# Infini-attention beside an FNet block on one core: value loads later in SyncE's order, chunk loads spread over the value tiles, the low memory products behind eight projection terms

## The chip, the cores and the metric

The kernel runs on 1 core of one Trainium2 chip. The metric is the device time of one execution in microseconds; the median of 3 runs before the change is 1089.74 us (1086.66 to 1097.31). One further execution was profiled; every duration below comes from it.

## The reference

Two independent blocks are computed from 2048 x 576 inputs in float32, and their results stand side by side in the output.

```python
# A: attention with a compressive memory: 32 heads of 18 columns, 4 segments of 512 rows
q, k, v = x @ wq, x @ wk, x @ wv
for s in range(4):
    logits = qs @ ks.T * scale + mask          # the mask adds -1e9 where key column > query row
    a_dot  = softmax(logits) @ vs
    a_mem  = (phi(qs) @ M) / (phi(qs) @ z + 1e-6)
    o      = g * a_mem + (1 - g) * a_dot       # g = sigmoid(beta), one per head
    M, z   = M + phi(ks).T @ vs, z + sum(phi(ks))
out_A = concat(o) @ wo
# B: real part of a DFT over the hidden and then the sequence axis
a, b  = x @ hid_re.T, x @ hid_im.T
out_B = seq_re @ a - seq_im @ b
```

## The kernel before, in words

**Numbers as halves.** Float32 operands are split into a high part (an ACT copy to the matmul type) and a low part (a subtraction on DVE or POOL), and a product is made of three matmuls: high x low, high x high, low x high. So most loads are followed by a split before TensorE (PE) can use them. All engines run the program in the order in which it was written (the schedule is manual). Every DMA is issued by SyncE (SP), from one queue and in order: a DMA that has to wait for a buffer or for data holds back all the DMAs behind it.

**The order written by hand.** `later(n, fn)` puts a call n ticks ahead of now, and `tick()` (line 85) runs what is due. In the first stage a tick comes after each projection tile and each value tile. In the second stage a tick comes after each *piece* of attention, of which there are eight in each step p of `attention()` (line 804). After each tick the loop at line 864 also emits dense work until its share of the total has caught up.

**First stage, segments s = 0 to 3 (lines 433 to 477).** `open_qk(s)` runs the first four projection tiles: for s > 0 terms 0 to 5 of all four tiles, then `accumulate(3)`, then terms 6 to 13 of all four. `accumulate(3)` adds the last 128 rows of the segment before to the memory: three products (high keys x high values, high x low, low x high) of five matmuls each. Then `memory()` copies the memory out of PSUM on ACT and masks it on POOL. Nine calls of `project_qk` follow; each stores its tile to DRAM one or two ticks later. Then come four value tiles j: `project_v(s, j)` on PE, an evacuation to `vs` (two buffers, `vs_bufs[j % 2]`), a store `vd<-vs`, and for s > 0 `lookup(s, j)` with a store `amd<-am` (`am` has one buffer). In the last segment the loop also starts the second stage: from n = 6 on the stacks of group 0 are loaded, and the first chunks of the dense work are loaded by `c_load` (four `craw` buffers) and split by `c_cut` (chunk 0 at j = 1, chunk 1 at j = 2; later ones by `chunk(n)`, which loads chunk n + 4 and splits chunk n + 2).

**Second stage.** PE alternates attention and dense work (B's two DFTs: `hidden` and `sequence`). Attention takes 32 groups G of four heads; a group needs two steps p, so 16 pieces. With the ticks counted from the start of `attention()`, group G's events, all on SP unless another engine is named, are:

| tick | event |
|---|---|
| 16G - 15 to 16G - 13 | the twelve loads `qs<-qd` and `ks<-kd` of group G (`stack_load`, called in step 2(G - 1)) |
| 16G + 13 | PE: the last `pv` of group G - 2, last reader of its value tile |
| 16G + 15 | `vst<-vd`, the value tile of group G (two buffers, so it waits for that `pv`) |
| next piece | `ptt<-hl`, a DMA transpose (`f_turn`; one in each step p) |
| 16G + 16 | PE: transposes the row maxima of group G (`trm`); ACT copies them to `mt` |
| 16G + 17 | `md<-mt`, stores them to DRAM; then the twelve loads of group G + 2, up to tick 16G + 19 |
| 16G + 22 | `qs<-md`, loads the maxima back as extra rows of `qs` |
| 16G + 24 | PE: the first `t_fill` of group G (line 737), which reads those rows |
| 16G + 35 | PE: the first `pv` of group G, which reads the value tile |

The tick of the value load is `later(lag, values)` in `stack_load` (line 418), called at tick 16(G - 1) with a lag of 31. Group 0 has a lag of 99 of its own and is loaded before `attention()` starts. At the end, A's output projection runs on PE (lines 884 to 900).

Of the kernel before, what the change touches and what calls it, by code (L numbers as in the profile page):

```python
# [36 lines left out]
def infini_attention_and_fnet(ctx: ExitStack, tc: tile.TileContext, xT, wqk, w8, wv, wo, beta, xtT, cT, hT, out):  # L37
# [44 lines left out]
    def later(n, fn, *a):  # L82
        due.setdefault(clock[0] + n, []).append((fn, a))

    def tick():
        clock[0] += 1
        for fn, a in due.pop(clock[0], ()):
            fn(*a)  # L88
# [12 lines left out]
    def load_x(s, k):  # L101
        t = sb.tile([P, L], F32, name="raw", tag="raw", bufs=5) if s else sk.tile([P, L], F32, name="kf", bufs=5)
        dma(t, xT[k, :, s * L:(s + 1) * L])
        XR[s, k] = t
# [81 lines left out]
    for i in range(2):  # L186
        kn.append(tuple(sk.tile([P, D], F32R, name=f"kn{n}{i}") for n in "hl"))
        a, b = (sk.tile([P, H, 19], F32R, name=f"vn{n}{i}") for n in "hl")
# [17 lines left out]
    def qk_terms(s, m):  # L206
        xh, xl, xt = X[s]
        W, c = (WQ, m) if m < 4 else (WK, m - 4) if m < 8 else (W8, 0)
        cs = slice(c * P, (c + 1) * P)
        terms = []  # L210
        for k in range(4):
            terms += [(W[0][k][:, cs], xh[k]), (W[0][k][:, cs], xl[k]), (W[1][k][:, cs], xh[k])]
        return terms + [(W[2][:, cs], xt), (W[3][:, cs], xt)]
# [3 lines left out]
    def warm_up():  # L217
        o = ps.tile([P, 1024], F32, name="kt", bufs=1)
        for _ in range(44):
            pe.matmul(o[:, :P], ident16, ident16, start=True, stop=True)  # L220

    def open_qk(s):
        for m in range(4):
            FIRST[m] = ps.tile([P, L], F32, name="qk", tag="acc", bufs=4)
        terms = [qk_terms(s, m) for m in range(4)]
        edges = (0, 6, 14) if s else (0, 3, 6, 9, 14)
        for a, b in zip(edges, edges[1:]):
            for m in range(4):
                for n in range(a, b):
                    pe.matmul(FIRST[m], *terms[m][n], start=n == 0, stop=n == 13)  # L230
            if s and a == 0:
                accumulate(3)

    def project_qk(s, m):
        if m in FIRST:
            o = FIRST.pop(m)
        else:
            o = ps.tile([P, L], F32, name="qk", tag="acc", bufs=4)
            chain(o, qk_terms(s, m))
        if m >= 4 and s < 3:  # L240
            KF[m] = sk.tile([P, L], F32, name="kf", bufs=5)
            act.activation(KF[m], o, AF.Copy)
        p = sb.tile([P, 3, L], BF16, name="p", bufs=4)
        r = sb.tile([P, L], F32, name="r", bufs=2)
        act.activation(p[:, 0], o, AF.Copy)
        dve.tensor_tensor(r, o, p[:, 0], OP.subtract)
        if s and (m < 4 or m == 8):
            n = P if m < 4 else 64
            c = m if m < 4 else 4
            phi(sb, "q", o[:n], n, pq_hi[:n, c], pq_lo[:n, c])  # L250

        def rest():
            if m in (5, 6, 7):
                pool.tensor_copy(p[:, 1], r)
            else:
                act.activation(p[:, 1], r, AF.Copy)
            pool.tensor_tensor(p[:, 2], r, p[:, 1], OP.subtract)
            if m < 8:
                later(1, dma, (qd if m < 4 else kd)[s][(m % 4) * P:(m % 4 + 1) * P], p)
            else:  # L260
                later(1, dma, qd[s][4 * P:], p[:64])
                later(1, dma, kd[s][4 * P:], p[64:])

        later(1, rest)
# [36 lines left out]

    started = set()

    def accumulate(j):
        (kh, kl), (vh, vl) = kn[j % 2], vn[j % 2]
        for a, v in ((kh, vh), (kh, vl), (kl, vh)):
            for c in range(5):
                b = c // 3
                cs = slice(64 + c * P, 64 + (c + 1) * P) if c < 4 else slice(0, 64)
                o = m_ps[b][:cs.stop - cs.start, c % 3]  # L310
                hs = slice(HEAD0[c], HEAD0[c] + 8)
                pe.matmul(o, a[:, cs], v[:, hs], start=b not in started, stop=True, skip_group_check=True)
                started.add(b)

    def memory():
        mf = sk.tile([P, 5, 8, 19], F32, name="mf")
        act.activation(mf[:, :3], m_ps[0], AF.Copy)
        act.activation(mf[:, 3], m_ps[1][:, 0], AF.Copy)
        act.activation(mf[:64, 4], m_ps[1][:64, 1], AF.Copy)
        pool.memset(mf[64:, 4], 0.0)  # L320
        for c in range(5):
            base = P * c - DH * HEAD0[c]
            pool.affine_select(mf[:, c], mf[:, c], pattern=[[-DH, 8], [0, 19]], base=base,
                               channel_multiplier=1, compare_op=OP.is_ge, fill=0.0)
            pool.affine_select(mf[:, c], mf[:, c], pattern=[[DH, 8], [0, 19]], base=DH - 1 - base,
                               channel_multiplier=-1, compare_op=OP.is_ge, fill=0.0)
        later(4, split, md_hi, md_lo, mf)
# [30 lines left out]
    def h_load(ri, k):  # L358
        HRAW[ri, k] = sb.tile([P, D], F32, name="raw", tag="raw", bufs=5 if ri == 0 else 3)
        dma(HRAW[ri, k], hT[ri, k])  # L360

    def h_split(ri, k):
        if k == 0:
            HW[ri] = weight(wide_tile(D))
        split_wk(HW[ri], k, HRAW.pop((ri, k)), 2 * ri)
# [5 lines left out]
    def c_load(n):  # L371
        if n < len(CHUNKS) and n not in c_seen:
            c_seen.add(n)
            src, at, k = CHUNKS[n]
            t = sr.tile([P, 5, P], F32, name="craw", bufs=4)
            dma(t[:, :k], src[at])
            c_raw[n] = t
# [20 lines left out]
    def stacks(p_, i):  # L398
        qs_bufs.append(p_.tile([P, 4, L], BF16, name=f"qs{i}"))
        ks_bufs.append(p_.tile([P, 4, L], BF16, name=f"ks{i}"))  # L400
        pool.memset(ks_bufs[i].bitcast(F32)[96:], BF16_ONES)
# [13 lines left out]

    NG = 32

    def stack_load(G, lag=31):
        if G >= NG:
            return  # L420
        s, g8 = divmod(G, 8)
        rows = slice(g8 * 72, g8 * 72 + 72)
        for buf, src, parts in ((qs_bufs[G % 4], qd[s], QPARTS), (ks_bufs[G % 4], kd[s], KPARTS)):
            for c, part in enumerate(parts):
                later(1 + c // 2, dma, buf[18 * c:18 * c + 18],
                      src[rows, part, :].rearrange("(h d) t -> d h t", d=DH))

        def values():
            VS[G] = sa.tile([P, 4, 220], BF16, name="vst", bufs=2)
            dma(VS[G], vd[s][:, :, g8])  # L430
        later(lag, values)

    for s in range(NSEG):
        more = s < 3
        if s == 0:
            warm_up()
        open_qk(s)
        if s:
            memory()
        else:  # L440
            tick()
        for n, m in enumerate((0, 1, 2, 3, 8, 4, 5, 6, 7) if s else range(9)):
            project_qk(s, m)
            tick()
            if not more and n >= 5:
                h_split(0, n - 5)
            if s in (1, 2) and n >= 4:
                load_x(s + 1, n - 4)
            if not more and n == 0:
                for k in range(5):  # L450
                    h_load(0, k)
            if not more and n == 4:
                p1k.close()
                sr = ctx.enter_context(tc.tile_pool(name="sb2r", bufs=1, side="right", reuse_waits="tile"))
                attention_tiles()
            if not more and n in (5, 6):
                stacks(sr, n - 5)
            if not more and n in (5, 7, 8):
                c_load(max(n - 6, 0))
            if not more and n == 6:  # L460
                stack_load(0, 99)
        for j in range(4):
            project_v(s, j, lookup(s, j) if s else iter(()))
            if more:
                k_natural(j)
            tick()
            for k in ((0, 1), (2, 3), (4,), ())[j] if s == 0 else ():
                load_x(1, k)
            if more and j in (1, 2):
                split_x(s + 1, j - 1)  # L470
            if not more and j < 3:
                h_split(0, 4) if j == 0 else c_cut(j - 1, dve)
            if not more and j in (1, 2):
                c_load(2 + j)
            if more and j:
                accumulate(j - 1)
    p1.close()
# [326 lines left out]
    def attention():  # L804
        for p in range(NP + V_LAG):
# [14 lines left out]
            if p % 2 == 0:  # L820
                stack_load(p // 2 + 1)
# [112 lines left out]
```

## Time and profile before

| | |
|---|---|
| median of 3 runs | 1089.74 us |
| the profiled execution | 1086.32 us, span 1084.3 us |
| busy: PE, DVE, ACT, POOL | 1027.7, 764.8, 688.4, 627.3 us |
| mean granted TensorE clock | 0.989 |
| first stage | 0 to about 233 us |
| attention and dense work | about 233 to 1008 us |
| output projection | about 1010 to 1084 us |

A busy PE is not PE at its peak, since matmul ends are modelled. "PE t L737 <- DMA qs<-md: 34.0, 19, 4.3" means that matmuls of line 737 that write tile t waited 34.0 us in total for the DMA that writes qs from md, 19 times, at most 4.3 us. For SP a wait is measured from the end of its instruction before. The name behind the arrow is found from a semaphore's last update, and it can be another instruction of the same engine: "PE s L662" behind a wait of the value load is PE's progress, while the instruction really needed is `pv`.

### The profile page before, as it was taken

How to read it: one execution, taken by the hardware profiler on the slowest of the kernel's cores; microseconds unless marked ns; L12 is line 12 of the kernel's file. 1: busy time of each engine (PE TensorE's matmuls, PEld its weight loads, DVE VectorE, ACT ScalarE, POOL GpSimd, SP SyncE). 2: the span in 40 equal slices, each digit the busy share in tenths (PEclk: the TensorE clock that was granted, in tenths of full speed). 3: DMA queues.
4: the chain of work that ended last, by engine and by line, in shares of the span. 5: the costliest groups of instructions: out<-in, count | busy, mean ns of one | idle time of the engine just before them, and what ended most of it. 6: DMA issues, size and time to landing. Idle time of an engine off the chain costs nothing.

```text
span 1084.3 us, 25741 instructions
## 1 busy us (share of the span) xinstructions
PE 1027.7 (95%) x9464; PEld 950.0 (88%) x9464; DVE 764.8 (71%) x2095; ACT 688.4 (63%) x1462; POOL 627.3 (58%) x668
## 2 busy tenths in 40 slices
PE   9999999989998989988999999999899898899998
PEld 7989899888997978887988999988888888789998
DVE  6555555744786877778888788878788768696343
ACT  7656575645776766766776777756666656566233
POOL 3566675845755656656666776665566556557000
PEclk9999999999999999999999999999999999999999
DMA  7525153455677796777887777777878877978574
GB/s 256 162 86 191 71 201 129 162 198 169 137 166 183 193 189 177 176 192 204 209 201 181 194 198 181 180 187 166 211 189 200 218 198 169 210 172 186 138 204 142
DMA packets 287743, 194.45 MB, mean 179 GB/s; under 512 B 210497, under 2 KB 242817, under 8 KB 287617
## 3 DMA queue, kind: packets, MB, share of 16 engines
q1 hardware_dynamic: 287616, 192.81, 68.4%
q8 instruction: 74, 1.21, 0.5%
q14 instruction: 53, 0.43, 0.1%
HBM read 106.84 MB, written 43.97 MB: 139 GB/s over the span
## 4 chain that ended last, share of the span: by engine, by line
PE 62%; DMA 16%; DVE 7%; SPq 5%; ACT 4%; issue 3%; POOL 3%; POOLq 0%; DVEq 0%; ACTq 0%
PE d L491 20%; DMA qs<-md 7%; PE d L78 5%; PE qk L78 4%; PE v L78 4%; PE s L662 4%; DMA qs<-qd 4%; PE qk L230 3%; SPq L88 3%; PE d L537 3%; PE pv L779 3%; PE d L538 3%; PE d L539 3%; DMA craw<-cT 2%; DVE s L668 2%
## 5 line engine op out<-in xcount | busy, mean ns | idle before, releaser
L668 DVE CUSTOM_DVE_ANT_0 s<-s,causal 128x512 f32<-128x512 f32 (+3 forms) x512 | 253.4, 496 | 112.4 <-PE s L662 101.2
L391 POOL TENSOR_TENSOR clo<-craw,chi 128x512 fp32r<-128x512 f32 x158 | 210.7, 1334 | 180.9 <-ACT chi L386 156.9
L491 PE MATMUL d<-wide,chi 128*128 128x288 f32 x1408 | 267.2, 307 | 0.2 <-DVE y L559 0.2
L491 PEld LDWEIGHTS d<-wide,chi 128*128 128x128 f32 x1408 | 212.8, 191 | 5.8 <-issue 3.5
L491 PE MATMUL d<-wide,clo 128*128 128x288 f32 x704 | 177.6, 319 | 0.0
L691 ACT ACTIVATE pf<-s,nb 128x512 f32<-128x512 f32 (+3 forms) x256 | 127.4, 525 | 50.7 <-DVE nb L683 49.9
L662 PE MATMUL s<-ks,qs 108*128 108x512 bf16 (+3 forms) x512 | 135.1, 307 | 7.8 <-ACT pf L691 6.0
L747 ACT ACTIVATE phi<-t 128x384 f16<-128x384 f32 x128 | 62.7, 490 | 112.1 <-PE t L744 79.7
L702 POOL TENSOR_TENSOR hl<-pf,hl 128x768 f16<-128x768 f32 x64 | 110.8, 1731 | 38.2 <-ACT hl L698 32.4
L491 PE MATMUL d<-ab,chi 128*128 128x288 f32 x640 | 126.1, 306 | 0.0
L491 PEld LDWEIGHTS d<-wide,clo 128*128 128x128 f32 x704 | 118.6, 192 | 2.6 <-issue 0.6
L748 ACT ACTIVATE pf<-t 128x384 f32<-128x384 f32 (+1 forms) x192 | 100.0, 521 | 29.4 <-PE t L737 29.3
L762 DVE TENSOR_TENSOR plo<-pf,phi 128x384 f16<-128x384 f32 (+1 forms) x128 | 115.2, 900 | 0.0
L386 ACT ACTIVATE chi<-craw 128x512 fp32r<-128x512 f32 x160 | 100.5, 628 | 12.3 <-PE d L491 4.9
L491 PEld LDWEIGHTS d<-ab,chi 128*128 128x128 f32 x640 | 98.7, 191 | 1.2 <-issue 0.4
L698 ACT ACTIVATE hl<-pf 128x768 f16<-128x768 f32 (+1 forms) x128 | 87.4, 729 | 2.0
L491 PE MATMUL d<-ab,clo 128*128 128x288 f32 x320 | 85.0, 315 | 0.0
L537 PE MATMUL d<-wide,chi 128*128 128x288 f32 x256 | 83.5, 326 | 0.0
L762 POOL TENSOR_TENSOR plo<-pf,phi 128x384 f16<-128x384 f32 x64 | 63.3, 988 | 22.9 <-ACT pf L748 21.7
L538 PE MATMUL d<-wide,chi 128*128 128x288 f32 x256 | 75.7, 296 | 0.0
L539 PE MATMUL d<-wide,clo 128*128 128x288 f32 x256 | 75.6, 295 | 0.0
L702 DVE TENSOR_TENSOR hl<-pf,hl 128x512 f16<-128x512 f32 x64 | 60.2, 941 | 0.1
(196 smaller groups left out, 2537.4 us busy)
## 6 DMA issues: line engine op xcount, KB each, us to landing
craw<-cT SPq DMA_DIRECT2D x128, 256.0 KB
qs<-qd SPq DMA_DIRECT2D x192, 72.0 KB
ks<-kd SPq DMA_DIRECT2D x192, 72.0 KB
craw<-xtT SPq DMA_DIRECT2D x32, 320.0 KB
out<-y SPq DMA_DIRECT2D x31, 288.0 KB
vd<-vs SPq DMA_DIRECT2D x16, 440.0 KB
vst<-vd SPq DMA_DIRECT2D x32, 220.0 KB
qd<-p SPq DMA_DIRECT2D x16, 384.0 KB
```

Of the source, the lines that this page charges most:

```text
L78: pe.matmul(o, a, b, start=n == 0, stop=n == len(terms) - 1)
L386: act.activation(hi, raw[:, :4], AF.Copy)
L391: engine.tensor_tensor(lo, raw[:, :4], hi.bitcast(F32), OP.subtract)
L491: pe.matmul(o[h], a, b[:, h * 288:h * 288 + 288], start=start, stop=stop)
L537: pe.matmul(o, xh[:, k], wl[k][:, cs], start=k == 0, stop=False)
L538: pe.matmul(o, xh[:, k], wh[k][:, cs], start=False, stop=False)
L539: pe.matmul(o, xl[:, k], wh[k][:, cs], start=False, stop=False)
L662: pe.matmul(o[:, c:c + w], q[:, i * P:w], k[:, :w], start=True, stop=True)
L668: dve.tensor_tensor_reduce(o[:, c:c + w], o[:, c:c + w], CAUSAL[0][:, L - w:], scale=scale, scalar=-LOWEST, op0=OP.add, op1=OP.min, accum_ ...
L691: act.activation(f[:, FIRST_COL[i]:FIRST_COL[i] + w], o[:, c:c + w], AF.Exp, bias=nb[:, i:i + 1], scale=-1.0)
L702: engine.tensor_tensor(hl[:, 1, a:b], f[:, a:b], hl[:, 0, a:b], OP.subtract)
L762: (pool if kind == 2 else dve).tensor_tensor(lo[:, a:b], f[:, a:b], hi[:, a:b], OP.subtract)
```

## The change

Three edits. The lag of the value loads goes from 31 to 39 ticks, so `vst<-vd` of group G moves from tick 16G + 15 to 16G + 23. In the last segment chunk 0 is still loaded after the sixth projection tile, but chunks 1 to 4 are loaded one after each value tile (before: chunks 1 and 2 after the eighth and ninth projection tiles, chunks 3 and 4 after value tiles 1 and 2). In `open_qk`, for s > 0, the third product of `accumulate(3)` moves behind terms 6 to 13 of projection tile 0.

```diff
 open_qk
             for m in range(4):
                 for n in range(a, b):
                     pe.matmul(FIRST[m], *terms[m][n], start=n == 0, stop=n == 13)
+                if s and m == 0 and a:
+                    accumulate(3, (2,))
             if s and a == 0:
-                accumulate(3)
+                accumulate(3, (0, 1))
...
-    def accumulate(j):
+    def accumulate(j, which=(0, 1, 2)):
         (kh, kl), (vh, vl) = kn[j % 2], vn[j % 2]
-        for a, v in ((kh, vh), (kh, vl), (kl, vh)):
+        for a, v in [((kh, vh), (kh, vl), (kl, vh))[n] for n in which]:
...
-    def stack_load(G, lag=31):
+    def stack_load(G, lag=39):
...
-            if not more and n in (5, 7, 8):
-                c_load(max(n - 6, 0))
+            if not more and n == 5:
+                c_load(0)
...
-            if not more and j in (1, 2):
-                c_load(2 + j)
+            if not more:
+                c_load(1 + j)
```

## The prediction

> **What bounds the kernel now.** I read the waits first, PE's before all, because the page gives PE 95% of the span. In the stretch of attention and dense work (300 to 1000 us), PE waited for:
>
> ```profile
> PE t L737 <- DMA qs<-md: 34.0, 19, 4.3
> PE s L662 <- ACT pf L691: 6.0, 11, 1.1
> PE pv L779 <- DMA ptt<-hl: 2.1, 2, 1.1
> ```
>
> So nearly all of PE's idle time there is one wait, for the maxima that come back through DRAM, in 19 of 32 groups. They are issued by SP; its own waits in the same stretch begin with:
>
> ```profile
> SPq L430 <- PE s L662: 94.5, 24, 6.5
> ...
> SPq L430 <- PE d L491: 16.3, 4, 5.3
> ```
>
> L430 is the value load. Both rows are its wait for PE: 110.8 us in 28 groups, 4.0 us each. Does this delay the maxima? The timeline of SP for group 27 (start, duration, instruction), and PE behind it:
>
> ```profile
> 871.42 0.59 SPq L430 DMA_DIRECT2D vst<-vd  x1
> 872.09 0.56 SPq L376 DMA_DIRECT2D craw<-cT  x1
> 872.77 3.70 SPq L707 DMA_TRANSPOSE ptt<-hl  x1
> 876.56 0.49 SPq L88 DMA_DIRECT2D md<-mt  x1
> ...
> 884.79 0.77 SPq L88 DMA_DIRECT2D qs<-md  x1
> ...
> 889.03 0.49 PE L737 MATMUL t<-qs,ks 111*128 111x128 bf16 x4 [2.52 <-DMA qs<-md]
> ```
>
> SP's instruction before ended at 867.4; it stood at the value load for 4.0 us until the last `pv` that reads that buffer (its record ends at 871.39), then needed 3.7 us for the transpose, and stored the maxima at 876.56 although ACT had finished them at 874.02. From there SP works without a pause (twelve stack loads at some 0.37 us, others) to `qs<-md`, 8.2 us later, and PE goes on 4.2 us after that. So SP is the queue that ends last: between two value loads (22.7 us) it issues for about 18 us, and stands about 4 us at the load.
>
> Each such stop also costs clock. The granted clock is 0.5 for 3.41 us at seven places: six right after one of these waits (stops of 1.8 to 4.3 us), one in the first stage. The stretches of group 27 and of that seventh place show it (PE busy and PEclk are what to read):
>
> ```profile
> 889.00:892.50 3.50, 3.47 (x18) 3.15 (x17) 0.00 (x0) 0.60 (x1) 3.35 (x3) 0.52 0.98 242
> 892.50:896.00 3.50, 3.50 (x43) 3.18 (x42) 2.73 (x10) 1.98 (x5) 0.99 (x4) 0.99 0.18 68
> 226.98:230.39 3.41, 3.41 (x17) 3.41 (x16) 2.82 (x9) 1.84 (x4) 2.08 (x2) 0.50 0.74 246
> ```
>
> 18 matmuls against 43 in equal time. Each half-clock stretch loses 3.41 x 0.5 = 1.7 us. The Trainium skill ("TensorE: Matmul & The Clock Gate", Part 1) gives idling of about 3.4 us as what halves the clock; here five stops of 1.8 to 2.8 us did it and five others of 2.0 to 2.5 us did not, so the measurement decides. By that rule alone, one attention stop (4.28 us) would cost clock instead of six, and the sum below would be about 7 us smaller.
>
> In the first stage PE loses little, at two places. `accumulate(3)` waits for the low keys three times, and the last value tile 4.35 us for an evacuation that waits for the store of value tile 0, whose buffer it writes:
>
> ```profile
> 122.55 0.74 PE L312 MATMUL m<-vnh,knl 128*128 128x152 f32 x5 [0.25 <-POOL knl L204]
> ...
> 225.38 0.42 ACT L289 ACTIVATE vs<-v 128x288 bf16<-128x288 f32 x1 [6.91 <-DMA vd<-vs]
> ...
> 226.42 0.53 PE L78 MATMUL v<-wide,xh 128*128 128x288 f32 x2 [4.35 <-DVE vr L292]
> ```
>
> **Value loads eight ticks later.** No work is added or removed. The load moves from before one transpose, `md<-mt`, the twelve stack loads, an `od` store and some chunk and output transfers, to right behind `qs<-md` of its group. There, `pv` has been done for 11 us or more in the groups up to 29 (end of its records to the issue of `qs<-md`), so the wait is met. SP gains 4 us, but cannot use all of it. The transpose needs `hl`: its last write on POOL or DVE ended 1.1 to 4.1 us before the transposes in question. And `md<-mt` needs ACT's copy, done 0.6 to 5.4 us before the store. The smaller of the two per group is the advance: 1.8 us on average. Taken from the 19 stops one by one, it leaves 5.2 us of the 34.0, in groups 10, 21, 22 and 26 above all. That is 28.8 us if all of it reaches `qs<-md`. SP's short waits between the two (some 1 us a period, for DMAs under way) may eat some: with 0.9 us lost in every group half of the gain goes (14 us is left). At the other end the load's own 0.6 us, which also leaves the path, frees part of the 5.2: 31. I take 24, nearer to the rows of group 27, where nothing stands between.
>
> Clock: of six half-clock stretches I take five away, 5 x 1.7 = 8.5 (2 to 6: 3.4 to 10.2).
>
> What is late next: PE without stops meets DVE, ACT and POOL sooner. PE's wait for ACT's exponentials is 6.0 us in all; between 600 and 700 us, where PE is 99.7% busy, DVE is 83% and ACT 75%, so they can follow. I charge 3 us (0 to 8).
>
> Cover of the later load: the first `pv` of the group comes 15.4 to 23.5 us after `qs<-md`; the load needs some 4 to 6 us, by what `qs<-md` (4.2) and the value store below (6.3) took to be seen.
>
> **Chunk loads.** `vd<-vs` of value tile 0 is issued at 218.96 and landed at 225.3. Before it SP now issues chunks 1 and 2 (at 211.49 and 213.85, 0.8 us with gaps), and standing for DMAs under way costs it 2.2 us from 214.9 to 217.4. Without them it is bound by POOL's `vs`, which ends at 217.45: 1.0 to 1.5 us earlier. The 640 KB are also out of its way, 2.6 us at the 251 GB/s of that stretch (1.6 if their packets overlap better). Together 2.6 to 4.1 of the 4.35 us; I take 3.2. What is left is shorter than any stop that halved the clock: 1.7 us more (0 at the other end). Against it: chunk 4 now goes between the last value store and the stack loads of group 1, so chunk 5, for which ACT stands 3.7 us at 249.9 (PE 1.4 us), comes 0.4 to 1.5 us later; I charge 0.5. Chunks 1 to 3 still land microseconds before their splits. Sum 4.4 (2 to 6).
>
> **Low products.** Between the end of the second product and the third, PE loses 0.42 us three times; eight projection terms (1.8 us) now cover the wait: 1.2 us. But ACT's copy of the memory, ahead of tile 0's evacuation in ACT's order, comes some 1.4 us later, and that evacuation 0.4 us. It starts a chain of ACT and DVE that in the last segment leads to the POOL work above. I take 0.8 (-1.2 to 1.2).
>
> Sum: 24 + 8.5 - 3 + 4.4 + 0.8 = 34.7 us. From the profiled execution's 1086.3: 1051.6; from the median, 3.4 us higher: 1055.0. I forecast 1054.
>
> **Rivals.** (1) The queue hands the time on: SP leaves one wait only to stand for `hl`, `mt` and DMAs under way, and `qs<-md` moves by 0.5 us a group. For it: SP is 80% issue, and it will stand for `mt` again. Against it: in group 27 both were ready 2.5 us early. It gives 19 x 0.5 = 9.5 us at most and little clock, with 3 to 5 us from the first stage: 1076, or 1079 with the 3 us of new waits. Chance 0.10.
> (2) The transfer, not its issue, sets the stop: the 6 KB load needs 4.2 us because of the twelve stack loads ahead of it, and with them sooner in the queue it lands no sooner. Against it: those loads also move. Only the first stage pays: 1085, no change. Chance 0.04. The Trainium skill ("DMA: Bandwidth & Descriptors", Issuing engines are not separate DMA queues) calls issue time usually small beside the transfer, which points this way; here the transpose alone holds SP 3.7 us.
> (3) Slower: the value tile comes too late. It decides when the load takes over 15.4 us to land, or SP falls as far behind. Each microsecond beyond that stops PE in some 30 groups; 2 us over costs 60 against the 35 gained: 1115. Against it: nothing here lands in over 7 us. Chance 0.05. The same page (Rules for kernel authors) says to issue a DMA early and wait late, which speaks against this edit; here the early issue is what stands 4.0 us in the queue.
> (4) Half: a standing loss of 0.9 us a group, gain 14 + 3.4 - 3 + 4.4 + 0.8 = 19.6: 1070. Chance 0.15.
>
> **How the numbers follow.** Forecast 0.66 (1041 with every term at its better end, 48.4 us; 1065 with the largest at its worse). The range 1041 to 1078 takes in rival (4) and the better end of (1). A measurement can tell 1% from no change, 1078.8 to 1100.6. Half of (1) and all of (2) lie there: same 0.09; slower 0.05; faster 0.86.
>
> **What would show it.** SP's wait at L430 near 0; `md<-mt` within 0.5 us of the end of `mt` or of the transpose; PE's wait for `qs<-md` under 10 us; at most two half-clock stretches; the last value tile's stop under 1.5 us; no wait of L312. I am wrong if L430's wait comes back at `md<-mt` with PE's wait unchanged, or if PE waits for `vst`.

## The result, and the profile after

The changed kernel took 1049.44 us (median of 4 runs, 1045.25 to 1049.82), beside 1091.48 us for the kernel before (4 runs, 1086.66 to 1097.31): a ratio of 0.960, with a 95% interval of 0.955 to 0.966. The profiled execution took 1049.82 us, 36.5 us less than the one of before.

Where they come from is read between three places that both traces have: the `trm` transposes of groups 0 and 31 and the first matmul of the output projection.

| | before | after | gained |
|---|---|---|---|
| start to `trm` of group 0 (first stage, first pieces) | 253.61 | 251.86 | 1.75 us |
| to `trm` of group 31 | 718.4 | 683.7 | 34.7 us |
| to the output projection | 41.9 | 41.9 | 0.0 us |

(Lines below 229 of the code have moved by two: L662, L737, L779 are now L664, L739, L781, and L430 is L432. In the experiments lines are those of before, or one or two further down.) PE's waits of the changed kernel between 300 and 1000 us:

```profile
PE s L664 <- ACT pf L693: 9.3, 14, 2.2
PE t L739 <- DMA qs<-md: 2.6, 7, 0.7
PE pv L782 <- DVE plo L764: 2.6, 6, 1.2
```

The wait for the maxima is down from 34.0 to 2.6 us. The two others have grown, by 3.3 and 1.4 us: with PE earlier, ACT and DVE are late more often. Now SP in group 27, and the matmul that waits for it:

```profile
843.79 3.13 SPq L709 DMA_TRANSPOSE ptt<-hl  x1
847.01 0.50 SPq L88 DMA_DIRECT2D md<-mt  x1
...
854.43 0.73 SPq L88 DMA_DIRECT2D qs<-md  x1
855.92 0.33 SPq L378 DMA_DIRECT2D craw<-cT  x1
856.49 0.58 SPq L432 DMA_DIRECT2D vst<-vd  x1
...
859.58 0.38 PE L739 MATMUL t<-qs,ks 111*128 111x128 bf16 x4 [0.22 <-DMA qs<-md]
```

The transpose starts 0.15 us after the last write of `hl` (2.56 before), and `md<-mt` 0.13 us after ACT's copy (2.54 before). Over groups 2 to 29 `md<-mt` follows that copy by 0.32 us on average, where it was 2.17. SP stands at the value load for 0.4 us in all, from 113.8, counted from the end of SP's instruction before to the load's own start, over all groups. From `md<-mt` to `qs<-md` SP needs 7.4 us (8.2 before); over all groups the average is 6.9 us (7.0 before). So what went is the standing, and PE is stopped for 0.22 us instead of 2.52. Half-clock stretches after 300 us fell from six to one (at 824.4 us, behind a stop of 2.17 us for ACT).

One sum accounts for the 34.7 us. Between the two transposes PE's records leave 45.2 us idle before and 18.9 after; half of PE's busy time in half-clock stretches, taken as lost, is 9.9 us before and 1.7 after. That makes 34.5 us. What is left of the time is 663.3 us before and 663.1 after: PE's work itself did not change. In the experiments below this remainder is 662.1 to 663.1 us, except at a lag of 51 (655.5, which stays open). So the runs differ there by PE's stops and its clock.

In the first stage, PE in the changed kernel:

```profile
209.96 0.34 PE L339 MATMUL look<-mdl,pq_hi 128*128 128x152 f32 x1 [0.49 <-DVE r L248]
...
223.59 0.80 PE L78 MATMUL v<-wide,xh 128*128 128x288 f32 x2 [1.60 <-DVE vr L294]
...
249.83 0.40 PE L539 MATMUL d<-wide,chi 128*128 128x288 f32 x1 [0.93 <-DVE wide L56]
```

The stop at the last value tile has shrunk from 4.35 to 1.60 us, but two stops are new: 0.49 us at a lookup and 0.93 us at the fifth chunk. And the half-clock stretch stayed, although a stop of 1.60 us is shorter than any that had one before:

```profile
223.67:227.08 3.41, 3.41 (x15) 3.41 (x16) 3.19 (x8) 1.71 (x6) 1.60 (x2) 0.50 0.76 270
227.08:230.49 3.41, 3.41 (x30) 3.41 (x29) 0.46 (x1) 1.26 (x3) 1.07 (x1) 1.00 0.68 228
```

(Stretch, mean busy time, then PE, PEld, DVE, ACT, POOL with their instructions, granted clock, DMA share, GB/s: 15 matmuls against 30 in equal time.)

### The profile page after: what moved, and what is told of

The parts are those of the page before. It is cut to its first block, busy times and chain, and to the rows that moved or that the text cites. A ratio compares the mean times of both kernels' runs of the same rounds, so it can differ in the third digit from the quotient of the medians.

```text
span 1047.8 us, 25775 instructions
## 1 busy us (share of the span) xinstructions
PE 1019.4 (97%) x9464; PEld 942.9 (90%) x9464; DVE 769.6 (73%) x2095; ACT 687.1 (66%) x1462; POOL 632.0 (60%) x668
## 4 chain that ended last, share of the span: by engine, by line
PE 74%; DMA 9%; DVE 8%; ACT 3%; SPq 2%; issue 2%; POOL 2%; POOLq 0%; ACTq 0%; DVEq 0%
PE d L493 24%; PE qk L78 6%; PE d L78 6%; PE s L664 5%; PE qk L230 5%; PE v L78 5%; PE d L539 3%; PE pv L781 3%; PE d L540 3%; PE d L541 3%; DMA qs<-md 3%; DVE s L670 2%; DMA ptt<-hl 2%; DMA craw<-cT 2%; PE pv L782 2%; SPq L88 2%
## 5 line engine op out<-in xcount | busy, mean ns | idle before, releaser
L393 POOL TENSOR_TENSOR clo<-craw,chi 128x512 fp32r<-128x512 f32 x158 | 213.1, 1349 | 168.3 <-ACT chi L388 135.8
L493 PEld LDWEIGHTS d<-wide,chi 128*128 128x128 f32 x1408 | 209.6, 189 | 6.0 <-issue 3.6
L664 PE MATMUL s<-ks,qs 108*128 108x512 bf16 (+3 forms) x512 | 133.8, 304 | 11.2 <-ACT pf L693 9.3
L704 DVE TENSOR_TENSOR hl<-pf,hl 128x512 f16<-128x512 f32 x64 | 63.6, 994 | 0.1
```

The source lines that it names most:

```text
L393: engine.tensor_tensor(lo, raw[:, :4], hi.bitcast(F32), OP.subtract)
L493: pe.matmul(o[h], a, b[:, h * 288:h * 288 + 288], start=start, stop=stop)
L664: pe.matmul(o[:, c:c + w], q[:, i * P:w], k[:, :w], start=True, stop=True)
L704: engine.tensor_tensor(hl[:, 1, a:b], f[:, a:b], hl[:, 0, a:b], OP.subtract)
```

## The experiments

Each edit is to the kernel before, unless it says otherwise. "Stretch" is the time between the transposes of groups 0 and 31: 718.4 us before, 683.7 us in the change.

### One edit at a time

**The lag alone.**

```diff
-    def stack_load(G, lag=31):
+    def stack_load(G, lag=39):
```

> The kernel before with a lag of 39 and nothing else. Theory: almost the whole gain is this edit, by the wait that SyncE no longer has ahead of the maxima. From the transpose of the maxima of group 0 to that of group 31 the traces took 718.4 us before (253.61 to 972.00) and 683.7 us after (251.86 to 935.55), 34.7 us less. Expected here: 682 to 688 us for that stretch, PE's wait for qs<-md under 6 us, at most two half-clock stretches after 300 us, the transpose of group 0 still at 253.6, and a time of 0.966 to 0.971 of before. Rival (the three edits help each other, for instance because the first stage ends earlier): less than 25 us in that stretch.

Measured: 1051.04 us, ratio 0.963 (0.958 to 0.969); stretch 684.3 us; no half-clock stretch after 300 us; `trm` of group 0 at 253.94. PE's waits between 300 and 1000 us begin:

```profile
PE t L737 <- DMA qs<-md: 7.4, 7, 1.4
PE s L662 <- ACT pf L691: 7.0, 13, 1.1
PE pv L780 <- DVE plo L762: 2.6, 6, 1.2
```

The wait for the maxima is a little above the 6 us expected, and the ratio a little better than the 0.966 to 0.971 expected; the rest came as the theory had it. The lag alone accounts for 34.1 of the 34.7 us of the stretch, and the rival (the edits need each other) falls.

**The chunk loads alone.**

```diff
-            if not more and n in (5, 7, 8):
-                c_load(max(n - 6, 0))
+            if not more and n == 5:
+                c_load(0)
...
-            if not more and j in (1, 2):
-                c_load(2 + j)
+            if not more:
+                c_load(1 + j)
```

> The kernel before with the chunk loads of the last segment spread over the value tiles, and nothing else. Theory: vd<-vs of value tile 0 is issued at about 217.4 instead of 218.96 and lands some 3 us earlier, so PE's stop of 4.35 us falls to about 1.2 us; but chunk 5 comes later and PE loses 0.5 to 1 us more before the transpose of the maxima of group 0, which comes at 252.3 to 253.0 (before 253.61). The half-clock stretch at about 225 us may stay. No change in the waits of the attention stretch (qs<-md 28 to 40 us). Rival: chunk 5's delay takes all of it back, and the transpose stays at 253.6 or later.

Measured: 1090.65 us, ratio 0.998 (0.995 to 1.002): not to be told from no change. PE at the two places:

```profile
223.42 0.53 PE L78 MATMUL v<-wide,xh 128*128 128x288 f32 x2 [1.69 <-DVE vr L292]
...
248.08 0.40 PE L537 MATMUL d<-wide,chi 128*128 128x288 f32 x1 [0.89 <-DVE wide L56]
```

`vd<-vs` of tile 0 went out at 217.12, the stop fell by 2.66 us, and the stop of 0.89 us at the fifth chunk came with this edit. The `trm` of group 0 came at 250.10, 3.5 us earlier and outside what was expected, because this time no half-clock stretch followed the stop of 1.69 us. (One began at 250.7, behind the next two stops.) So 1.8 of the 3.5 us are the stops and 1.7 the clock, and the clock's part is handed back by the later half-clock stretch, which lies behind the `trm`. The attention stretch gained nothing: it took 727.9 us, `qs<-md` cost PE 36.8 us, and there were eight half-clock stretches. This is 9.5 us more than in the kernel before, whose order is the same there, and measures how far single executions scatter.

**The low products alone.**

```diff
+                if s and m == 0 and a:
+                    accumulate(3, (2,))
             if s and a == 0:
-                accumulate(3)
+                accumulate(3, (0, 1))
```

> The kernel before with the low product behind eight projection terms, and nothing else. Theory: PE gains 0.2 to 0.4 us in each of three segments (0.7 us together by the end of the third open_qk, where projection tile 1 starts at 183.4 instead of 184.1), but the store of value tile 0 is set by the chain over ACT, DVE and POOL, which does not gain, so PE's stop before the last value tile grows from 4.35 to about 5 us and the transpose of the maxima of group 0 stays at 253.4 to 253.8. Rival: that chain gains as PE does, and the transpose comes at 252.8 to 253.0.

Measured: 1090.85 us, ratio 1.000 (0.997 to 1.003).

```profile
183.31 0.44 PE L230 MATMUL qk<-xh,wide 128*128 128x512 f32 x1
...
210.06 0.34 PE L339 MATMUL look<-mdl,pq_hi 128*128 128x152 f32 x1 [0.49 <-DVE r L248]
...
225.79 0.85 PE L78 MATMUL v<-wide,xh 128*128 128x288 f32 x2 [3.71 <-DVE vr L294]
```

PE goes on with projection tile 1 of the last segment at 183.31 (183.92 before), so 0.6 us are gained there. The stop at the lookup is new and comes with this edit (the runs without it have none): PE, earlier, meets a DVE chain that is not. The last value tile begins 0.63 us earlier. Expected was a longer stop there (about 5 us); it is shorter, and 0.49 us of it has moved ahead. But the half-clock stretch then lasted from 224.3 to 231.1, two windows of 3.41 us instead of one, and `trm` of group 0 came at 253.94, no earlier than before (253.61). The stretch took 720.4 us. What the edit is worth without the clock, at most those 0.6 us, can't be told from this.

### The wait or the place?

The lag moves the load out of the way of the maxima in two senses: its wait is met, and its issue (0.6 us) and bytes go behind `qs<-md`. A third buffer takes the wait away and leaves the place; a lag of 33 takes the wait away and puts the load directly ahead of `md<-mt`.

```diff
-            VS[G] = sa.tile([P, 4, 220], BF16, name="vst", bufs=2)
+            VS[G] = sa.tile([P, 4, 220], BF16, name="vst", bufs=3)
...
-        w = sa.tile([24, P], BF16, name="mt", bufs=2)
+        w = sa.tile([24, P], BF16, name="mt", bufs=1)
...
-        a = sa.tile([P, 8, DH], F32, name="pa", bufs=2)
+        a = sa.tile([P, 8, DH], F32, name="pa", bufs=1)
```

> The kernel before with a lag of 31 as it was, but three buffers for the value tiles instead of two (room for it is made by one buffer instead of two for two small tiles, one of which only DVE uses and one that is used every 22 us). The load stays in its old place in SyncE's order, and has nothing to wait for. Theory (the in-order wait is what costs): as good as the lag of 39 within 6 us, that is 0.966 to 0.975 of before, with PE's wait for qs<-md under 8 us. Rival (what counts is that the load's issue time and bytes go behind qs<-md): at most 5 us gained, PE's wait for qs<-md above 25 us.

Measured: 1051.73 us, ratio 0.963 (0.957 to 0.969); stretch 686.3 us; the value load never waits; PE's wait for the maxima:

```profile
PE t L737 <- DMA qs<-md: 10.1, 9, 2.6
```

A little more than the 8 us expected, but the stretch lost 32.1 of the 34.1 us that the lag took from it, with the load where it always was. The wait is the cause.

```diff
-    def stack_load(G, lag=31):
+    def stack_load(G, lag=33):
```

> The kernel before with a lag of 33 alone: the value load goes one piece behind the transpose, directly ahead of md<-mt, so its 0.6 us of issue and its bytes stay ahead of the maxima, but pv is done by then. Theory (the wait is what costs, and two ticks are enough to lose it): SyncE's wait at the value load under 5 us in total, 684 to 692 us from the transpose of group 0 to that of group 31 (lag of 39: 684.3), 0.962 to 0.972 of before. Rival (the load must go behind qs<-md): 700 us or more for that stretch.

Measured: 1058.07 us, ratio 0.970 (0.966 to 0.974); stretch 691.7 us, just inside; no wait at the value load; and

```profile
PE t L737 <- DMA qs<-md: 15.5, 13, 2.8
```

So the place counts too, but less: 26.7 us of the stretch came with the wait, and up to 7.4 more with the place (a lag of 39). The third buffer's load is also ahead of the maxima, but it goes out ahead of the transpose, at which SP then stands until 0.15 us after `hl` in most groups; directly ahead of `md<-mt` nothing covers its 0.6 us, and the wait for the maxima is twice that of the lag of 39. On average `md<-mt` follows ACT's copy by 0.75 us (0.46 with the lag of 39) and `qs<-md` follows `md<-mt` by 7.3 us (7.0), together the load's 0.6 us. That the place counts is more than scatter: the four executions took 1057.05 to 1061.79 us, and those with a lag of 47, run beside them, 1043.59 to 1050.26. How many microseconds of the stretch it is stays open, since 7.4 us are within the 9.5 by which single executions differ.

### How late is too late?

> The kernel before with a lag of 47 alone: the value load comes four pieces ahead of its first pv in the written order, instead of twelve. Theory: SyncE runs some 3 us ahead of PE at that place (it then stands at the transpose for hl), so the load still has about 8 to 12 us until its pv and lands in 4 to 6: as good as a lag of 39, 682 to 690 us for the stretch, with no wait of pv for vst. The first prediction's third rival (too late) would show here as pv waiting for vst in most groups, and 700 us or more.

Measured (`lag=47`): 1049.10 us, ratio 0.960 (0.956 to 0.964); stretch 677.1 us, better than expected; PE waits 4.4 us for the maxima, never for the value tile. From the issue of the load to the first `pv` it took 9.2 to 17.0 us (15.1 to 22.7 in the change, 27.6 to 38.3 before).

> The kernel before with a lag of 51 alone: the value load comes in the same piece as its first pv, behind md<-mt and eight stack loads in SyncE's queue. Theory (this is where the load is too late): pv waits for vst in about 30 groups, 3 to 6 us each, 90 to 180 us in total, and most of these stops also start a half-clock stretch of 1.7 us; 800 to 900 us for the stretch, slower than before. If SyncE were so far ahead that even this is in time, the stretch stays under 700 us.

Measured (`lag=51`): 1202.82 us, ratio 1.102 (1.094 to 1.109); stretch 835.1 us. PE's waits between 300 and 1200 us:

```profile
PE pv L779 <- DMA vst<-vd: 113.5, 30, 6.8
PE s L662 <- ACT pf L691: 6.4, 12, 1.1
```

The wait for the maxima has gone from the list, and 3.8 us in each of 30 groups have come in its place, with 25 half-clock stretches after 300 us. `pv` followed the issue of its load by 3.6 to 5.6 us, which is now about how long the load takes to be seen. So the least lead that does no harm lies between some 6 and 9 us, as far as these runs show, and the change's 15 us or more left room.

### Better than both?

**The change without its low products** (a lag of 39 and the chunk loads).

> The change without its low products: a lag of 39 and the chunk loads spread over the value tiles. Theory: the low products bring nothing to the end (alone they left the transpose of group 0 where it was), so this is as fast as the whole change within 3 us: 0.958 to 0.966 of before; the transpose of group 0 between 250 and 252.3 us, depending on whether a half-clock stretch follows PE's stop at the last value tile. Rival (the low products are worth the 0.7 us that PE gains): 0.7 us slower in that place.

Measured: 1048.46 us, ratio 0.960 (0.955 to 0.964); stretch 683.3 us; `trm` of group 0 at 251.42, PE's stop at the last value tile 1.77 us, half-clock stretch only from 250.4 on. It is as fast as the whole change; the 0.7 us of the rival are too little to be told.

**The change with a lag of 47.**

> The whole change with a lag of 47 instead of 39. With a lag of 47 alone the stretch from the transpose of group 0 to that of group 31 took 677.1 us, with 39 alone 684.3; the load then stands ahead of a transpose for which SyncE waits anyway, instead of between qs<-md and the other transpose. If that place is worth it, the stretch takes 675 to 680 us here (whole change: 683.7) and the time is 0.952 to 0.959 of before. If the 7 us were one execution's luck, the stretch takes 682 to 686 us and the time is that of the change, 0.960 within 0.004.

Measured: 1048.83 us, ratio 0.959 (0.955 to 0.962); stretch 685.5 us. The 677.1 us of the other run were one execution's luck. PE stood idle 14.9 us in that stretch and lost nothing to the clock; here it stood 18.8 us and lost 4.6. From 39 to 47 the lag makes no difference that these runs can tell.

**A lag of 47, no low products, chunk 4 earlier.**

```diff
-            if not more and j in (1, 2):
-                c_load(2 + j)
+            if not more and j < 3:
+                for n in ((1,), (2, 3), (4,))[j]:
+                    c_load(n)
```

> A lag of 47, no low products, and another spread of the chunk loads: chunk 1 after value tile 0, chunks 2 and 3 after tile 1, chunk 4 after tile 2 (the change: 1, 2, 3, 4 after tiles 0 to 3). Theory: the stop of 0.9 to 1.5 us that PE makes in the change at the fifth chunk (about 249.8 us) comes from chunk 4's load standing between the last value store and the stack loads of group 1; here it goes, PE's stop at the last value tile stays 1.5 to 1.8 us, and the transpose of group 0 comes at 249.2 to 250.8. Time as the run beside it, or up to 1.5 us less. Rival (the later chunk 5 comes from somewhere else): the stop stays.

Measured: 1046.49 us, ratio 0.956 (0.953 to 0.959); stretch 682.6 us; `trm` of group 0 at 249.58, with no half-clock stretch in the first stage. PE at the places in question:

```profile
223.69 0.53 PE L78 MATMUL v<-wide,xh 128*128 128x288 f32 x2 [1.57 <-DVE vr L292]
...
249.58 0.23 PE L721 MATMUL trm<-ident,mb 128*128 128x128 bf16 x1 [1.38 <-POOL mb L716]
```

The stop at the fifth chunk is gone (1.50 us in the change without its low products, 1.96 in the change with a lag of 47), as expected of a chunk 4 that no longer goes out between the last value store and the stack loads. It is the fastest of all by its median, but its interval overlaps that of the change.

## Why the prediction was right, step by step

Forecast 1054, measured 1049.44; of the sum, 34.7 us against 36.5 between the two profiled executions. That they are so close is in part luck, for two errors cancel: the attention stretch was forecast at 24 + 8.5 - 3 = 29.5 us and gave 34.7; the first stage at 4.4 + 0.8 = 5.2 us and gave 1.75.

- **SP's wait as the cause.** Right, and shown from two sides: with the wait gone by a third buffer or by the lag, the stretch loses 32 to 34 us; with the lag of 33 that leaves issue and bytes ahead, still 26.7.
- **The advance is limited by `hl` and `mt`.** Right: SP now stands at the transpose until 0.15 us after `hl`, and the 5.2 us of waiting that the row-by-row sum left are 2.6 us in the change and 7.4 us with the lag alone.
- **24 us of the 34.0.** Sized too low. The allowance for SP's short waits between `md<-mt` and `qs<-md` was not needed: that way takes 6.9 us on average against 7.0. The lag alone took 26.6 us off this wait, the whole change 31.4, as high as the upper end. But the profiled execution of the change is the best of six with a lag of 39 or 47, in which 2.6 to 8.9 us of this wait are left.
- **Five of six half-clock stretches.** Right: all six behind waits for the maxima are gone; the one that is left follows a wait for ACT, and the lag alone left none.
- **3 us of new waits.** Near: PE's waits for ACT and DVE grew by 5 us in the change (exponentials 6.0 to 9.3, `plo` 1.2 to 2.6, `negm` 1.3 to 1.7).
- **Chunk loads, 4.4 us.** The mechanism was right: `vd<-vs` went out 1.59 us earlier and was seen 2.8 us earlier (225.3 to 222.5), which took 2.75 us off the stop against the 3.2 taken. The failed step is the clock: "what is left is shorter than any stop that halved the clock". The stop of 1.60 us did halve it, because all of it fell into one window (see below). Chunk 5's delay cost 0.9 us, not 0.5.
- **Low products, 0.8 us.** Failed; nothing was seen to reach the end. The term was also read too high: the trace before shows the wait for the low keys in two segments (122.55 and 181.45), not three. In segment 1 the third product starts at 63.73, 0.51 us after the second, as the second (63.22) starts 0.48 us after the first. The caveat was the right half: PE gains, the chain over ACT and DVE does not, and a new stop at the lookup takes 0.49 us back. The change without them is as fast.
- **The rivals.** (1) and (2) fell with the lag alone. For (1) the queue was read as fuller than it is: SP issues for 16.9 of 23.2 us per group on average, 73%, not for 18 of 22.7. (4) fell too: there is no standing loss between `md<-mt` and `qs<-md`. (3), the value tile too late, is a real mechanism that this change does not reach: its load goes out 15.1 us or more ahead of its `pv` and takes 4 to 6. At a lag of 51 the lead is 3.6 to 5.6 us; PE waits 113.5 us for the value tile, and the time is 10% above before.
- **What would have shown it wrong.** Its main figures held. The last value tile's stop is 1.60 us, not under 1.5, and in five groups (5, 22, 23, 25 and 29) another DMA of the queue stands between the transpose and `md<-mt`, which then follows both by 0.7 us or more.

The half-clock stretches could not be forecast from the lengths of stops alone. In each trace they start on a grid of 3.41 us: the first three before begin at 226.98, 404.47 and 725.32, 52 and 94 windows of 3.4133 us apart. What precedes them is a window of this grid in which PE stood idle for about half of the time or more. Two stops of equal length in the kernel before, 2.52 us each, show it (PE busy is the first number behind the comma):

```profile
401.06:404.47 3.41, 0.89 (x9) 0.60 (x8) 1.92 (x5) 2.24 (x5) 1.52 (x1) 1.00 1.08 170
...
745.80:749.22 3.42, 2.16 (x16) 1.92 (x15) 3.28 (x10) 2.14 (x4) 2.88 (x2) 1.00 1.13 201
749.22:752.63 3.41, 2.14 (x19) 2.00 (x18) 1.19 (x3) 1.07 (x3) 0.65 (x2) 1.00 1.02 223
```

The first fell into one window, with 2.52 us idle, and the clock halved at 404.47; the second was cut in two, with 1.26 and 1.27 us, and it did not. Over the twelve traces (without the first 30 and the last 20 us of each), all 64 windows at full clock with 1.82 us or more idle were followed by half clock; of the 14 between 1.60 and 1.82 us two were, one of them the change's 1.60; below 1.60 us none was. A half-clock window was followed by another when PE stood idle 0.63 us or more in it, and never below 0.58. So what a stop costs depends on where it falls in the grid, which no length tells.

The Trainium skill ("TensorE: Matmul & The Clock Gate", Part 1) says that the window which decides runs freely and does not start with the kernel. The runs agree: an edge of the grid lies at 223.67 us in the change and at 222.18 in the change with a lag of 47. At the same place, stops of 1.57, 1.60, 1.69 and 1.77 us were followed by no half clock, by one at once, and by none until 250 us (twice). The first and the last were cut by an edge; the 1.60 and 1.69 us lay almost or all in one window, at the border where either came.

## What to carry to other kernels

On a queue that issues in order, a load is best put behind the event that frees its buffer, not as early as its data exist: here a prefetch with 30 us of lead held up a 6 KB transfer with no lead at all. So look for a wait that does no harm to the transfer that waits, and ask which transfers stand behind it; a third buffer or a later place removes it nearly equally well. Then count the lead the other way too: here between 9 and 23 us of it made no difference that the runs can tell, and at 4 to 6 us the kernel was 10% slower than before.

## What the runs showed that was not expected

The half clock came after stops as short as 1.60 us, and after some of 1.7 to 2.5 us it did not come. Two short stops can also add up: in the run with the chunk loads alone, stops of 0.89 and 1.36 us left PE idle for 2.2 us of the window from 247.24, and half clock followed. One such stretch more or less moves the first stage by 1.7 us, so a gain of a microsecond there can't be read from one execution. And a DMA transpose holds SP for 3.0 to 5.8 us of issue, against 0.3 to 0.8 us for most other DMAs: in the kernel before, two of them are 7.7 of the 16.9 us that SP issues per group on average.
